# The sign bit of sixteen decoded weight pieces, set on another engine

## The chip, the cores and the metric

The kernel runs on one core of one Trainium2 chip. The metric is the device time of one execution in microseconds (us); the time before is 899.84 us, the median of 3 runs (899.83 to 900.71).

The engines that matter are TensorE (PE: matrix products), VectorE (DVE) and ScalarE (ACT), each with its own in-order queue of instructions, and the DMA queue of SyncE (SP), which loads inputs and stores the result. An instruction waits in its queue until semaphores say that what it reads has been written and that what it overwrites is no longer needed.

## The reference

Attention inside chunks of 64 rows, followed by a two-layer network whose activation is a rational function. The weights arrive as 64-bit floats, the rest as 32-bit floats.

```python
# attention, for each chunk of 64 rows, head_dim 64
scores = scale * q_c @ k_c.T
attn = softmax(scores)            # along the last axis, + 1e-9 in the divisor
x = attn @ v_c                    # 4608 tokens x 512
# network: w_in 512 x 2048, w_out 2048 x 512, a has 4 numbers, b has 2
h = x @ w_in
P = a[0] + a[1] * h + a[2] * h**2 + a[3] * h**3
Q = 1.0 + abs(b[0]) * abs(h) + abs(b[1]) * h**2
out = (P / (Q + 1e-06)) @ w_out   # float32
```

## The kernel before

**Tiling.** The 4608 tokens are 18 blocks n of 256. For each block there is one attention part, and then four steps s of 512 hidden columns. Steps are numbered g; for the first two blocks they alternate (g = 0 is block 0, step 0; g = 1 is block 1, step 0; g = 2 is block 0, step 1, and so on up to g = 7), after that they run block by block. A step g consists of the first product (`F g`, `f g` on TensorE, line 332, into the PSUM tile `ph`), the rational function, twelve instructions on ScalarE and VectorE with letters of their own (among them `p` and `P`, lines 360 and 364, of which `P` is VectorE's last read of `ph`; `g`, line 369, which writes `ghi`; `G`, line 381, which writes `glo`), and the second product (`Z g`, `z g` from `ghi`, `y g` from `glo`; line 407, into `po`). Each operand of a product is split into a high and a low part, and three products of the parts are summed.

**The weights.** They are decoded on the chip from the 64-bit floats. There are 16 pieces j of 128 x 1024 numbers, 8 of `w_in` and 8 of `w_out`, each loaded by one DMA (`w j`) into one of three buffers `raw` as pairs of 32-bit words, the low word first. A piece then goes through these instructions:

- `o j` (line 149, VectorE): the low word is shifted right by 29, which leaves its upper three bits;
- `s j` (line 153, ScalarE): the high word, read as a 32-bit float, is scaled by 2^-111. That moves its exponent and keeps its sign;
- the sign, in one of two ways. `i j` (line 157, ScalarE) converts the scaled high word to a 16-bit float and writes it into the upper half of the low word; the number is so small that only the sign is left of it. `e j` (line 161, VectorE) ands the high word with the sign mask and ors it into the low word, both 32 bits wide;
- `j j` (line 165, VectorE): the high word is shifted left by 3 and the low word ored in;
- `h j` (line 168, ScalarE): the high part for the products. The low part comes either from `d j` (line 173, VectorE) or from two products with identity matrices, `r j` on TensorE, and `l j` on ScalarE.

A `raw` buffer is free for the next load when `d j` or `r j` has read it.

**The order.** The first twelve steps are interleaved with the attention of blocks 0 to 3 and with the decoding by a table written out by hand, `START`: each entry is a letter and a piece, step or block number (with a half, as in `N0.1`), and the instructions are issued in the order of the table, each to the queue of its engine. Attention letters that matter here: `S` scores (TensorE, tile `pss`), `M` row maximum (VectorE, line 241), `U`, `E` and `n` subtraction, exponential and sums, `N` normalisation (VectorE, line 275), `T` transposition (TensorE, `pst`), `K` copy (ScalarE, line 288), `A` product with v (TensorE, `psx`), `X` and `Y` its high and low part (ScalarE, line 311, and VectorE, line 315). From step 12 on a loop issues the rest, without decoding.

In the table, pieces 1, 4, 2, 12, 7 and 10 take their sign by `e`, the other ten (3, 0, 5, 8, 6, 9, 13, 11, 14, 15) by `i`.

Of the kernel before, what the change touches and what calls it, by code (L numbers as in the profile page):

```python
# [13 lines left out]
ALU = mybir.AluOpType  # L14
# [16 lines left out]
EXP_WIDE = (0, 1)  # L31

START = (
# [12 lines left out]
)  # L46
FIRST = 12
CUT_FIRST, CUT_LAST = 24, 48
# [6 lines left out]
def tile_chunked_attention_rational_moe(  # L55
# [11 lines left out]
    nc = tc.nc  # L67
    cp = ctx.enter_context(tc.tile_pool(name="cp", bufs=1))
    p2 = ctx.enter_context(tc.tile_pool(name="p2", bufs=2))
# [14 lines left out]
    a0, a1, a2, a3 = (ab[:, i:i + 1] for i in range(4))  # L84
    b0, b1a = ab[:, 4:5], ab[:, 6:7]
# [36 lines left out]
    raws, pls = {}, {}  # L122
# [17 lines left out]
    def words(j):  # L140
        low, high = raws[j][:, :, 0], raws[j][:, :, 1]
        return low, high, high.bitcast(F32)
# [10 lines left out]
        nc.scalar.activation(val, val, AF.Copy, scale=2.0 ** -111)  # L153

    def w_sign(j):
        upper = raws[j].bitcast(mybir.dt.float16).rearrange("p f (w h) -> p f w h", h=2)[:, :, 0, 1]
        nc.scalar.copy(upper, words(j)[2])

    def w_sign_dve(j):
        low, high, _ = words(j)  # L160
        nc.vector.scalar_tensor_tensor(low, high, -(2 ** 31), low, ALU.bitwise_and, ALU.bitwise_or)  # L161

    def w_join(j):
        low, high, val = words(j)
# [297 lines left out]
    def qk(n, u=None):  # L462
# [5 lines left out]
    of_step = lambda f: lambda g: f(*steps[g])  # L468
    do = {
        "k": consts, "B": abs_b1, "q": qk, "v": load_v, "w": w_load,  # L470
        "o": w_low, "s": w_scale, "j": w_join, "i": w_sign, "e": w_sign_dve, "h": w_hi, "d": w_lo_dve, "r": w_rest, "l": w_lo,
        "S": att_s, "M": att_max, "U": att_sub, "E": att_exp, "n": att_rs, "N": att_norm,
        "T": att_t, "K": att_copy, "A": att_av, "X": att_xhi, "Y": att_xlo,
        "O": store,
# [22 lines left out]
    for g in range(FIRST, total + LAG):  # L497
        n, s = steps[min(g, total - 1)]
# [66 lines left out]
```

## Time and profile before

| | |
|---|---|
| median of the timed runs | 899.84 us (899.83 to 900.71) |
| span of the profiled execution, first to last instruction | 898.1 us |
| the profiled execution's own time | not listed apart from its span; the median is 1.7 us above the span |
| mean granted TensorE clock | 0.996 |
| busy time PE, PEld (weight loads) | 870.1 us, 854.2 us |
| busy time DVE, ACT | 748.0 us, 581.9 us |
| decoding: last instruction of it starts at | 129.4 us |

The profile is of one execution. A row of the timeline gives start, duration, engine, line, operation, what is written and read, and in brackets the idle time of the engine before it and what ended it. Durations of neighbours on one engine overlap by some tens of nanoseconds to a tenth of a microsecond, because the next instruction starts while the last one drains; what an instruction takes from its queue is therefore the distance from its start to the next start, called its slot below.

### The profile page before, as it was taken

How to read it: one execution, taken by the hardware profiler on the slowest of the kernel's cores; microseconds unless marked ns; L12 is line 12 of the kernel's file. 1: busy time of each engine (PE TensorE's matmuls, PEld its weight loads, DVE VectorE, ACT ScalarE, POOL GpSimd, SP SyncE). 2: the span in 40 equal slices, each digit the busy share in tenths (PEclk: the TensorE clock that was granted, in tenths of full speed). 3: DMA queues.
4: the chain of work that ended last, by engine and by line, in shares of the span. 5: the costliest groups of instructions: out<-in, count | busy, mean ns of one | idle time of the engine just before them, and what ended most of it. 6: DMA issues, size and time to landing. Idle time of an engine off the chain costs nothing.

```text
span 898.1 us, 21079 instructions
## 1 busy us (share of the span) xinstructions
PE 870.1 (97%) x9390; PEld 854.2 (95%) x9390; DVE 748.0 (83%) x671; ACT 581.9 (65%) x981; POOL 0.8 (0%) x8
## 2 busy tenths in 40 slices
PE   2699999999999999999999999999999999999998
PEld 2498999999999999999999999999999999999998
DVE  6999997898878878787878897878787878878784
ACT  6899987676656566665747475757565656566452
POOL 0000000000000000000000000000000000000000
PEclk9999999999999999999999999999999999999999
DMA  8525432103030303030201111020202030101010
GB/s 303 213 96 188 168 115 51 69 1 95 2 95 1 95 2 94 1 94 2 65 32 29 68 25 72 17 81 1 95 2 95 1 95 2 48 1 25 1 24 25
DMA packets 16506, 55.88 MB, mean 62 GB/s; under 512 B 2592, under 2 KB 2592, under 8 KB 14368
## 3 DMA queue, kind: packets, MB, share of 16 engines
q1 hardware_dynamic: 16256, 54.28, 18.5%
q8 instruction: 74, 1.21, 0.5%
q10 hardware_dynamic: 160, 0.26, 0.1%
q14 instruction: 16, 0.13, 0.0%
HBM read 45.09 MB, written 9.44 MB: 61 GB/s over the span
## 4 chain that ended last, share of the span: by engine, by line
PE 93%; DVE 3%; DMA 1%; ACT 1%; issue 1%; SPq 0%; ACTq 0%; DVEq 0%
PE ph L332 43%; PE po L407 42%; PE psx L205 2%; PE pss L205 2%; PE pst L284 2%; PE pe L407 1%; DMA Bqk<-in_kT 1%; PE pl L181 1%; DMA raw<-in_w_out 1%; DVE raw L165 0%; PE pe L432 0%; PE po L432 0%; DVE C L360 0%; DVE C L364 0%; DVE raw L161 0%
## 5 line engine op out<-in xcount | busy, mean ns | idle before, releaser
L332 PE MATMUL ph<-xhi,wi_hi 128*128 128x256 f32 x1152 | 322.7, 280 | 6.8 <-DVE C L364 6.8
L332 PE MATMUL ph<-xlo,wi_hi 128*128 128x256 f32 x1152 | 319.8, 278 | 0.0
L332 PE MATMUL ph<-xhi,wi_lo 128*128 128x256 f32 x1152 | 319.5, 277 | 0.0
L337 ACT ACTIVATE A<-ph,ab 128x1024 f32<-128x1024 f32 x72 | 80.7, 1121 | 253.9 <-PE ph L332 253.2
L332 PEld LDWEIGHTS ph<-xhi,wi_hi 128*128 128x128 f32 x1152 | 217.3, 189 | 8.3 <-ACT raw L153 7.5
L407 PE MATMUL po<-wo_hi,ghi 128*128 128x256 f32 (+1 forms) x1112 | 220.4, 280 | 0.0
L332 PEld LDWEIGHTS ph<-xlo,wi_hi 128*128 128x128 f32 x1152 | 217.7, 189 | 0.1
L332 PEld LDWEIGHTS ph<-xhi,wi_lo 128*128 128x128 f32 x1152 | 217.5, 189 | 0.0
L407 PE MATMUL po<-wo_lo,ghi 128*128 128x256 f32 x1112 | 217.1, 276 | 0.0
L348 DVE SCALAR_TENSOR_TENSOR B<-B,ab,A 128x1024 f32<-128x1024 f32 x72 | 92.4, 1283 | 99.0 <-ACT B L340 99.0
L407 PEld LDWEIGHTS po<-wo_hi,ghi 128*128 128x128 f32 x1112 | 167.6, 188 | 2.3 <-issue 0.3
L407 PEld LDWEIGHTS po<-wo_lo,ghi 128*128 128x128 f32 x1112 | 167.6, 188 | 0.0
L407 PE MATMUL po<-wo_hi,glo 128*128 128x256 f32 (+1 forms) x1112 | 138.1, 277 | 0.1
L407 PEld LDWEIGHTS po<-wo_hi,glo 128*128 128x128 f32 x1112 | 131.5, 188 | 0.3 <-DVE glo L381 0.3
L369 DVE SCALAR_TENSOR_TENSOR ghi<-C,ab,A 128x1024 fp32r<-128x1024 f32 x72 | 92.4, 1283 | 10.8 <-ACT A L356 2.4
L352 ACT ACTIVATE A<-B,cst 128x1024 f32<-128x1024 f32 x72 | 83.1, 1155 | 24.8 <-DVE B L348 24.7
L377 DVE SCALAR_TENSOR_TENSOR B<-C,ab,B 128x1024 f32<-128x1024 f32 x72 | 92.3, 1283 | 2.3
L364 DVE SCALAR_TENSOR_TENSOR C<-C,ab,ph 128x1024 f32<-128x1024 f32 x72 | 92.1, 1280 | 2.1
L381 DVE TENSOR_TENSOR glo<-B,A 128x1024 fp32r<-128x1024 f32 x72 | 88.2, 1224 | 6.6
L360 DVE TENSOR_TENSOR C<-C,ph 128x1024 f32<-128x1024 f32 x72 | 87.4, 1214 | 4.2 <-ACT B L340 3.6
L344 ACT ACTIVATE C<-ph,ab 128x1024 f32<-128x1024 f32 x72 | 87.6, 1216 | 4.5 <-PE ph L332 4.5
L373 DVE SCALAR_TENSOR_TENSOR B<-B,ghi 128x1024 f32<-128x1024 f32 x72 | 88.2, 1224 | 2.3
(72 smaller groups left out, 737.3 us busy)
## 6 DMA issues: line engine op xcount, KB each, us to landing
v<-in_vP SPq DMA_DIRECT2D x18, 512.0 KB, 4.1
out<-o SPq DMA_DIRECT2D x68, 128.0 KB, 2.4
raw<-in_w_in SPq DMA_DIRECT2D x8, 1024.0 KB, 6.1
raw<-in_w_out SPq DMA_DIRECT2D x8, 1024.0 KB, 4.8
qk<-in_qT SPq DMA_DIRECT2D x16, 512.0 KB, 4.8
qk<-in_kT SPq DMA_DIRECT2D x16, 512.0 KB, 5.6
Aqk<-in_qT SPq DMA_DIRECT2D x2, 256.0 KB, 5.3
Bqk<-in_kT SPq DMA_DIRECT2D x2, 256.0 KB, 5.8
```

The costliest lines, as they stand in the source:

```text
L332: nc.tensor.matmul(ph[:, fi, :], w[:, cc, f], x[:, cc, :], start=(k == 0), stop=(k == len(mm) - 1))
L337: nc.scalar.activation(ch[n, s][1], ch[n, s][0], AF.Abs, scale=b0)
L344: nc.scalar.activation(ch[n, s][3], ch[n, s][0], AF.Identity, bias=a2, scale=a3)
L348: nc.vector.scalar_tensor_tensor(B, B, b1a, A, ALU.mult, ALU.add)
L352: nc.scalar.activation(A, B, AF.Ln, bias=cst[:, 0:1], scale=2.0 ** -KLN)
L360: nc.vector.tensor_mul(C, C, h)
L364: nc.vector.scalar_tensor_tensor(C, C, a1, h, ALU.add, ALU.mult)
L369: nc.vector.scalar_tensor_tensor(gbuf[n, s][0], C, a0, A, ALU.add, ALU.mult)
L373: nc.vector.scalar_tensor_tensor(B, B, CQ, gbuf[n, s][0].bitcast(F32), ALU.add, ALU.mult)
L377: nc.vector.scalar_tensor_tensor(B, C, a0, B, ALU.add, ALU.subtract)
L381: nc.vector.tensor_mul(gbuf[n, s][1], B, A)
L407: nc.tensor.matmul(accs[n][i][:, cols], g[:, fi, i * 128:(i + 1) * 128], w[:, FPS * s + fi, cols], start=start, stop=stop,)
```

## The change

All 16 pieces now take their sign in one way. `i j` is a VectorE instruction with one operand: it reads the upper 16 bits of the high word as an integer, ands them with the sign mask, and writes them into the upper 16 bits of the low word. Elements are 16 bits wide, and successive ones are 8 bytes apart in reading and writing. `e` is gone, and in the table each `e j` is replaced by `i j` in its place; nothing else in the table changes (the diff shows it re-wrapped).

```diff
 START = (
...
-    ... w4 e1 T0.1 ... Y0.1 e4 j4 ... f0 e2 E1 ...
+    ... w4 i1 T0.1 ... Y0.1 i4 j4 ... f0 i2 E1 ...
...
     def w_sign(j):
-        upper = raws[j].bitcast(mybir.dt.float16).rearrange("p f (w h) -> p f w h", h=2)[:, :, 0, 1]
-        nc.scalar.copy(upper, words(j)[2])
-
-    def w_sign_dve(j):
-        low, high, _ = words(j)
-        nc.vector.scalar_tensor_tensor(low, high, -(2 ** 31), low, ALU.bitwise_and, ALU.bitwise_or)
+        half = raws[j].bitcast(mybir.dt.int16).rearrange("p f (w h) -> p f w h", h=2)
+        nc.vector.tensor_scalar(half[:, :, 0, 1], half[:, :, 1, 1], -(2 ** 15), None, ALU.bitwise_and)
...
-        "o": w_low, "s": w_scale, "j": w_join, "i": w_sign, "e": w_sign_dve, "h": w_hi, "d": w_lo_dve, "r": w_rest, "l": w_lo,
+        "o": w_low, "s": w_scale, "j": w_join, "i": w_sign, "h": w_hi, "d": w_lo_dve, "r": w_rest, "l": w_lo,
```

Four lines fewer stand ahead of what follows, so line 165 of before is line 161 after, line 364 is 360, and so on; line 157 is the new sign instruction.

VectorE's queue has 10 rows more, ScalarE's 10 fewer; PE's and SP's orders stay. Three places of VectorE's queue follow; numbers behind tile names tell buffers apart.

The first is early, during the attention of block 0: `raw_107` is piece 0, `raw_116` piece 1, `raw_86` piece 3; `e_111` being normalised is `N0.1`. Before:

```order
L173 SCALAR_TENSOR_TENSOR wi_lo<-raw_86,wi_hi 128x4x256
L275 TENSOR_TENSOR e_111<-e_111,sm_109 128x2x4x64
L161 SCALAR_TENSOR_TENSOR raw_116<-raw_116 128x1024
L165 SCALAR_TENSOR_TENSOR raw_107<-raw_107 128x1024
L165 SCALAR_TENSOR_TENSOR raw_116<-raw_116 128x1024
```

and now:

```order
L169 SCALAR_TENSOR_TENSOR wi_lo<-raw_86,wi_hi 128x4x256
L157 TENSOR_SCALAR raw_107<-raw_107 128x1024
L271 TENSOR_TENSOR e_111<-e_111,sm_109 128x2x4x64
L157 TENSOR_SCALAR raw_116<-raw_116 128x1024
L161 SCALAR_TENSOR_TENSOR raw_107<-raw_107 128x1024
L161 SCALAR_TENSOR_TENSOR raw_116<-raw_116 128x1024
```

The sign of piece 0 came from ScalarE's queue and now stands ahead of `N0.1`; the sign of piece 1 stays where it was, in the other form.

The second is the rational function of step 0, up to `P0` (the last row). `raw_265` is piece 5. Before:

```order
L275 TENSOR_TENSOR e_300<-e_300,sm_294 128x2x8x64
L348 SCALAR_TENSOR_TENSOR B_0_342<-B_0_342,ab,A_0_341 128x1024
L360 TENSOR_TENSOR C_0_345<-C_0_345,ph_0_268 128x1024
L165 SCALAR_TENSOR_TENSOR raw_265<-raw_265 128x1024
L364 SCALAR_TENSOR_TENSOR C_0_345<-C_0_345,ab,ph_0_268 128x1024
```

and now:

```order
L271 TENSOR_TENSOR e_300<-e_300,sm_294 128x2x8x64
L157 TENSOR_SCALAR raw_265<-raw_265 128x1024
L344 SCALAR_TENSOR_TENSOR B_0_342<-B_0_342,ab,A_0_341 128x1024
L356 TENSOR_TENSOR C_0_345<-C_0_345,ph_0_268 128x1024
L161 SCALAR_TENSOR_TENSOR raw_265<-raw_265 128x1024
L360 SCALAR_TENSOR_TENSOR C_0_345<-C_0_345,ab,ph_0_268 128x1024
```

The sign of piece 5 has come in ahead of the rational function of step 0.

The third is around `P3` (the last row), VectorE's last read of the `ph` tile of step 3. `raw_640` is piece 9, `raw_672` piece 10. Before:

```order
L369 SCALAR_TENSOR_TENSOR ghi_0_706<-C_0_642,ab,A_0_627 128x1024
L360 TENSOR_TENSOR C_1_682<-C_1_682,ph_1_600 128x1024
L373 SCALAR_TENSOR_TENSOR B_0_628<-B_0_628,ghi_0_706 128x1024
L149 TENSOR_SCALAR raw_672<-raw_672 128x1024
L364 SCALAR_TENSOR_TENSOR C_1_682<-C_1_682,ab,ph_1_600 128x1024
```

and now:

```order
L365 SCALAR_TENSOR_TENSOR ghi_0_706<-C_0_642,ab,A_0_627 128x1024
L356 TENSOR_TENSOR C_1_682<-C_1_682,ph_1_600 128x1024
L369 SCALAR_TENSOR_TENSOR B_0_628<-B_0_628,ghi_0_706 128x1024
L157 TENSOR_SCALAR raw_640<-raw_640 128x1024
L149 TENSOR_SCALAR raw_672<-raw_672 128x1024
L360 SCALAR_TENSOR_TENSOR C_1_682<-C_1_682,ab,ph_1_600 128x1024
```

The sign of piece 9 has come in two rows ahead of `P3`.

24 rows, old and new, of the table START are left out of this document.

## The prediction

> **What bounds the kernel now.** I read the page first, then the busy time by stages, then the chain that ended last, then the rows around the places where TensorE waits.
>
> ```profile
> span 898.1 us, 21079 instructions
> PE 870.1 (97%) x9390; PEld 854.2 (95%) x9390; DVE 748.0 (83%) x671; ACT 581.9 (65%) x981; POOL 0.8 (0%) x8
> ```
>
> TensorE is busy for 870.1 of 898.1 us, so the time is its work plus 28 us of idling. Shares over the whole span hide where that lies; the stages show it (columns: busy us of PE, PEld, DVE, ACT, POOL, with instruction counts, then the granted clock, the DMA share and GB/s):
>
> ```profile
> 10.00:44.00 34.00, 19.14 (x229) 13.68 (x230) 31.86 (x39) 29.81 (x30) 0.00 (x0) 0.96 0.68 257
> 44.00:78.00 34.00, 34.00 (x307) 31.53 (x307) 33.90 (x33) 32.51 (x31) 0.00 (x0) 0.94 0.43 148
> 78.00:131.00 53.00, 53.00 (x555) 51.48 (x554) 52.75 (x51) 48.99 (x68) 0.00 (x0) 1.00 0.38 145
> 131.00:176.00 45.00, 45.00 (x496) 44.60 (x495) 36.09 (x33) 31.47 (x58) 0.00 (x0) 1.00 0.20 60
> 176.00:898.00 722.00, 717.78 (x7779) 711.94 (x7777) 591.11 (x515) 436.87 (x797) 0.00 (x0) 1.00 0.13 40
> ```
>
> From 44 us on TensorE hardly idles. VectorE is full from 10 to 131 us: it idles 2.14 us in the first of these stages (34.00 - 31.86), 0.10 in the second and 0.25 in the third. ScalarE is well filled too, but has 4.2, 1.5 and 4.0 us free. So while the weights are decoded VectorE is the engine without room, and from 131 us on it has plenty (8.9 us idle of 45). What VectorE gains or loses in the decoding reaches the end only where TensorE waits for it. The longest such wait, and its two sides:
>
> ```profile
> PE ph L332 <- DVE C L364: 6.8, 1, 6.8
> ...
> 42.31 1.27 DVE L364 SCALAR_TENSOR_TENSOR C<-C,ab,ph 128x1024 f32<-128x1024 f32 x1
> ...
> 43.73 0.55 PE L332 MATMUL ph<-xhi,wi_hi 128*128 128x256 f32 x1 [6.84 <-DVE C L364]
> ```
>
> `P0` on VectorE ends at 42.31 + 1.27 = 43.58, and 0.15 us later TensorE starts `F2`, which needs that `ph` tile. I take 0.15 us as the distance from a VectorE end to the TensorE start that it releases.
>
> **The change part by part.** The five decoding groups as they are (duration in ns: least, median, most):
>
> ```profile
> L149 DVE TENSOR_SCALAR raw<-raw x16: 643/687/696, 9.1 to 122.7; 128x1024 int32<-128x1024 int32 x16
> L153 ACT ACTIVATE raw<-raw x16: 1112/1185/1385, 9.1 to 118.0; 128x1024 f32<-128x1024 f32 x16
> L165 DVE SCALAR_TENSOR_TENSOR raw<-raw x16: 1212/1220/1226, 13.8 to 126.9; 128x1024 int32<-128x1024 int32 x16
> L157 ACT CAST raw<-raw x10: 2474/2608/2690, 10.7 to 124.0; 128x1024 f16<-128x1024 f32 x10
> ...
> L161 DVE SCALAR_TENSOR_TENSOR raw<-raw x6: 1214/1219/1227, 18.9 to 87.2; 128x1024 int32<-128x1024 int32 x6
> ```
>
> Removed from ScalarE: 10 x 2.608 = 26.1 us. Of this I count nothing: VectorE idles only 2.14 + 0.10 + 0.25 = 2.5 us between 10 and 131 us, so an earlier ScalarE can hardly release it earlier, and TensorE's wait above ends on VectorE. What covers it is VectorE's own queue; if that cover went, the most to come back would be these 2.5 us.
>
> On VectorE six two-operand signs go and sixteen new ones come. What counts is the slot:
>
> ```profile
> 18.25 0.68 DVE L275 TENSOR_TENSOR e<-e,sm 128x512 f32<-128x512 f32 x1
> 18.85 1.22 DVE L161 SCALAR_TENSOR_TENSOR raw<-raw 128x1024 int32<-128x1024 int32 x1
> 19.99 1.22 DVE L165 SCALAR_TENSOR_TENSOR raw<-raw 128x1024 int32<-128x1024 int32 x1
> ...
> 60.44 0.69 DVE L149 TENSOR_SCALAR raw<-raw 128x1024 int32<-128x1024 int32 x1
> 61.04 1.27 DVE L364 SCALAR_TENSOR_TENSOR C<-C,ab,ph 128x1024 f32<-128x1024 f32 x1
> ```
>
> An old sign takes 19.99 - 18.85 = 1.14 us of the queue. The new one is not in the trace. Its nearest row is L149: the same operation with one operand and a constant, the same 1024 elements at the same 8-byte steps, in place, only 32 bits wide; its slot is 61.04 - 60.44 = 0.60 us. The nearest rows that write 16-bit elements at 8-byte steps are ScalarE's L157, 2.2 times as long as L153 with 32 bits, and its slot is here:
>
> ```profile
> 77.79 2.63 ACT L157 CAST raw<-raw 128x1024 f16<-128x1024 f32 x1
> 80.07 1.30 ACT L153 ACTIVATE raw<-raw 128x1024 f32<-128x1024 f32 x1
> ...
> L249 DVE TENSOR_SCALAR sm<-sm x16: 170/174/177, 107.8 to 802.2; 128x16 f32<-128x16 f32 x16
> ```
>
> So 80.07 - 77.79 = 2.28 us is the upper end for the new slot. For the lower end: L249, the same operation on 16 elements, lasts 0.174 us, so of L149's 0.687 some 0.51 is for the elements; at twice the rate the slot would be about 0.60 - 0.26 = 0.34 us. I call the slot s and take s = 0.60, after L149, because engine, operation, count and steps agree, and L157 differs in engine.
>
> VectorE's total grows by 16 x 0.60 - 6 x 1.14 = 2.8 us. Where it arrives:
>
> ```profile
> 19.08 1.09 PE L284 MATMUL pst<-ident,e 128*128 128x128 f32 x4 [3.98 <-DVE e L275]
> ...
> 27.82 1.16 PE L205 MATMUL pss<-Bqk,Aqk 64*64 64x64 f32 x64
> ...
> 29.05 1.23 DVE L241 TENSOR_REDUCE sm<-pss 128x16 f32<-128x1024 f32 x1
> ```
>
> *Up to the restart of TensorE.* The sign of piece 3 falls into VectorE's idle time at 10 us (the wait for ScalarE's exponential), nothing. The sign of piece 0 stands ahead of `N0.1` (the row at 18.25), which TensorE's `T0.1` waits for at 19.08. Everything behind hangs on that as a chain (copy, product with v, high part, correction product, then `S1`): `S1` ends at 27.82 + 1.16 = 28.98, now + 0.60 = 29.58, and `M1`, at 29.05 before, is late by 0.53. (The pieces 1 and 4 are cheaper, but `M1` waits for `S1` now.) Behind `M1` VectorE runs without a gap: piece 2 gives back 1.14 - 0.60 = 0.54, piece 5 ahead of step 0 adds 0.60. `P0` and with it `F2` come 0.53 - 0.54 + 0.60 = **0.59 us** late.
>
> *From there to 131 us* TensorE and VectorE both run without gaps, and TensorE is late by the most that VectorE's delay exceeds the slack at a place where it takes something from VectorE:
>
> ```profile
> 78.49 1.27 DVE L364 SCALAR_TENSOR_TENSOR C<-C,ab,ph 128x1024 f32<-128x1024 f32 x1
> ...
> 79.95 0.31 PE L332 MATMUL ph<-xhi,wi_hi 128*128 128x256 f32 x1
> ...
> 116.93 1.22 DVE L381 TENSOR_TENSOR glo<-B,A 128x1024 fp32r<-128x1024 f32 x1
> ...
> 119.32 4.02 PE L407 MATMUL po<-wo_hi,glo 128*128 128x256 f32 x32
> ...
> 130.52 1.22 DVE L381 TENSOR_TENSOR glo<-B,A 128x1024 fp32r<-128x1024 f32 x1
> 132.36 1.22 DVE L360 TENSOR_TENSOR C<-C,ph 128x1024 f32<-128x1024 f32 x1 [0.62 <-ACT A L337]
> 133.50 1.22 DVE L315 TENSOR_TENSOR xlo<-psx,xhi 128x1024 fp32r<-128x1024 f32 x1
> 134.68 1.28 DVE L364 SCALAR_TENSOR_TENSOR C<-C,ab,ph 128x1024 f32<-128x1024 f32 x1
> ...
> 135.45 1.16 PE L205 MATMUL pss<-qk 64*64 64x64 f32 x64
> 136.54 0.39 PE L332 MATMUL ph<-xhi,wi_hi 128*128 128x256 f32 x1
> ...
> 148.48 1.22 DVE L360 TENSOR_TENSOR C<-C,ph 128x1024 f32<-128x1024 f32 x1 [2.11 <-ACT B L340]
> ```
>
> - `P3` (78.49) ends at 79.76; `F5` starts at 79.95: slack 0.04 after the 0.15. Pieces 12, 8, 7, 6, 9 lie between: -0.54 + 0.60 - 0.54 + 0.60 + 0.60 = 0.72, so `P3` is late by 1.31 and `F5` by 1.27.
> - `G4` (116.93) ends at 118.15; `y4` starts at 119.32: slack 1.02. Pieces 13, 10, 11, 14 add 1.26, 2.57 in all; `y4` late by 1.55.
> - Piece 15 makes it 3.17. `p6` started at 132.36 although VectorE was free at 130.52 + 1.13; those 0.71 us are absorbed, 2.46 remain. `Y2` (133.50) ends at 134.72 and releases `S3` at 135.45: slack 0.58, late by 1.88. `P6` ends at 135.96, `F8` starts at 136.54: slack 0.43, late by **2.03**.
>
> The other places where TensorE takes something from VectorE before 131 us have more slack, read off in the same way. Afterwards VectorE's idle time (2.11 us before the row at 148.48) takes up the delay, and VectorE follows TensorE. TensorE has no such idle time, so 2.03 us stay to the end. SP's order stays: a weight load starts when L173 or the correction product has released its buffer, and that shifts with its VectorE readers. For any s between 0.60 and 2.28 the same walk gives 13 s - 5.77.
>
> Span 898.1 + 2.0 = 900.1; the same 1.7 us as now between span and median give 899.84 + 2.03 = **901.9 us**.
>
> **The rivals.** *The 16-bit store is slow on VectorE too.* For it: L157 is the only 16-bit row with these steps and is 2.2 times as long as its 32-bit neighbour. Against: another engine, and L165, L149 and L153 do not suffer from 8-byte steps. At 2.2 x 0.60 = 1.32, 13 s - 5.77 = 11.4 us, 911.2 us; at one element a pass like the two-operand forms, s = 1.14, 9.1 us, 908.9; at ScalarE's own 2.28, 23.9 us, 923.7. [...]
>
> *Not slower: 16 bits run at double rate.* Then s = 0.34: `F2` would come at 3 x 0.34 - 1.21 = -0.2, the later places gain as well, and TensorE's own work holds the rest: 899.7 us. By 13 s - 5.77 the delay falls under 1.80 us, 0.2%, from s = 0.58 down. For it: the data are half as wide. Against: the sum of L149 is for elements, and the elements are as many and as far apart. [...]
>
> *ScalarE's relief counts.* If VectorE's idle 2.14 us before 44 went with it, the restart would come 1.55 us early instead of 0.59 late; the 1.44 us that come later (2.03 - 0.59) come all the same, in all -0.1, 899.7 us. I put it with the last.
>
> **How the numbers follow.** A measurement of this kernel tells 0.2% (1.8 us) from no change. Forecast, s near 0.60 (0.55 to 0.67, with the slacks read to some tenths): 901.0 to 903.0, chance 0.60, of which two thirds lie above 901.64 (0.40 slower, 0.20 same). Slow 16-bit stores: 0.22 for 909 to 911, 0.10 for 920 and more, all slower. Not slower, both ways: 0.08 (0.05 same, 0.03 faster). Together slower 0.72, same 0.25, faster 0.03. The range leaves out the 0.10 at the top and most of the 0.08 at the bottom: 900.2 to 911.3.
>
> **What would show it.** In the profile after: the duration of line 157 on DVE (0.69 for the forecast; 1.2 and more for the first rival, about 0.43 for the second); `F2`'s start near 44.3 instead of 43.73; new waits of `ph` line 328 at `F5` and `F8` for line 360; VectorE without gaps to about 134; ScalarE's busy time less by 26. The forecast is wrong if line 157 lasts something else, or if VectorE's slots elsewhere change once ScalarE stops writing 16-bit halves beside it.

## The result and the profile after

| | before | after |
|---|---|---|
| median of the timed runs | 900.24 us (899.83 to 900.71) | 909.12 us (908.89 to 909.62) |
| span of the profiled execution | 898.1 us | 907.1 us |
| sign on VectorE, median of one | 1.219 us (6, two-operand) | 1.342 us (16, 16-bit) |
| sign on ScalarE, median of one | 2.608 us (10) | none |
| VectorE, ScalarE busy over the span | 748.0, 581.9 us | 759.4, 559.7 us |

The ratio is 1.0098, 95% interval 1.0085 to 1.0112: slower by 8.9 us. (The 900.24 us are the median of four runs of the kernel before, one more than the 899.84 us above.) The new instruction and its neighbours in the decoding, as the view of the tile `raw` groups them after the change (least, median, most in ns):

```profile
L149 DVE TENSOR_SCALAR raw<-raw x16: 644/692/767, 8.9 to 132.1; 128x1024 int32<-128x1024 int32 x16
L157 DVE TENSOR_SCALAR raw<-raw x16: 1292/1342/1376, 10.1 to 133.9; 128x1024 int16<-128x1024 int16 x16
L161 DVE SCALAR_TENSOR_TENSOR raw<-raw x16: 1206/1226/1285, 13.9 to 137.4; 128x1024 int32<-128x1024 int32 x16
```

The same operation on the same 1024 elements at the same 8-byte steps lasts twice as long with 16-bit elements (line 157, 1.342 us) as with 32-bit ones (line 149, 0.692), and longer than the two-operand form (line 161, 1.226). Its slot, from the timeline after:

```profile
33.20 1.36 DVE L157 TENSOR_SCALAR raw<-raw 128x1024 int16<-128x1024 int16 x1
34.59 1.23 DVE L161 SCALAR_TENSOR_TENSOR raw<-raw 128x1024 int32<-128x1024 int32 x1
...
40.17 1.29 DVE L157 TENSOR_SCALAR raw<-raw 128x1024 int16<-128x1024 int16 x1
41.26 1.25 DVE L344 SCALAR_TENSOR_TENSOR B<-B,ab,A 128x1024 f32<-128x1024 f32 x1
...
121.44 1.34 DVE L157 TENSOR_SCALAR raw<-raw 128x1024 int16<-128x1024 int16 x1
122.55 1.25 DVE L369 SCALAR_TENSOR_TENSOR B<-B,ghi 128x1024 f32<-128x1024 f32 x1
```

The last two are 1.09 and 1.11 us, and all but two lie between 1.08 and 1.16; I use 1.12. The two are pieces 4 and 2, whose join `j` stands directly behind the sign: 1.37 and 1.39 us (the first pair of rows is piece 2), where the old sign took 1.26 and 1.25. At 1.12 each, the sixteen add 16 x 1.12 - 6 x 1.14 = 11.1 us to VectorE's queue. The stages after, in the columns of before:

```profile
10.00:44.00 34.00, 17.68 (x228) 12.90 (x228) 32.66 (x40) 20.77 (x25) 0.00 (x0) 0.94 0.69 259
44.00:78.00 34.00, 31.47 (x279) 28.84 (x280) 33.90 (x32) 25.40 (x25) 0.00 (x0) 0.91 0.30 105
78.00:131.00 53.00, 49.42 (x458) 46.95 (x457) 52.83 (x52) 38.52 (x64) 0.00 (x0) 1.00 0.39 142
131.00:176.00 45.00, 44.28 (x546) 43.48 (x544) 37.50 (x36) 29.30 (x56) 0.00 (x0) 1.00 0.30 95
176.00:907.00 731.00, 726.78 (x7855) 720.94 (x7853) 600.17 (x522) 443.29 (x803) 0.00 (x0) 1.00 0.13 40
```

VectorE is as full as before (33.90 of 34, 52.83 of 53). ScalarE fell from 32.51 to 25.40 and from 48.99 to 38.52, and nothing became faster by it. TensorE, which had no idle time from 44 to 176 us, now idles 2.5, 3.6 and 0.7 us there. The granted clock from 44 to 78 us reads 0.91 instead of 0.94, but that is no part of the loss: TensorE still stands idle for the first 2 us of that stage, and behind its restart the clock is 0.50 up to 50.1 us, for 4.0 us, against 4.4 us before (43.73 to 48.1). At single places, in the timeline of TensorE after, and two groups of its waits (us in total, times, longest):

```profile
46.11 0.55 PE L328 MATMUL ph<-xhi,wi_hi 128*128 128x256 f32 x1 [9.12 <-DVE C L360]
...
85.91 0.35 PE L328 MATMUL ph<-xhi,wi_hi 128*128 128x256 f32 x1 [1.29 <-DVE C L360]
...
144.87 1.16 PE L201 MATMUL pss<-qk 64*64 64x64 f32 x64
145.96 0.39 PE L328 MATMUL ph<-xhi,wi_hi 128*128 128x256 f32 x1
...
PE pst L280 <- DVE e L271: 6.0, 2, 5.1
PE po L403 <- DVE wo_lo L169: 1.1, 2, 0.7
```

`F2` starts 2.38 us late (43.73 before), `F5` 5.96 us (79.95), `S3` and `F8` 9.42 us (135.45 and 136.54), and the span ends 9.0 us late, so 0.4 us are made up behind `F8`. The loss grows through the decoding, piece by piece, and stops where the decoding stops.

### The profile page after: what moved, and what is told of

The parts are those of the page before. It is cut to its first block, busy times and chain, and to the rows that moved or that the text cites. A ratio compares the mean times of both kernels' runs of the same rounds, so it can differ in the third digit from the quotient of the medians.

```text
span 907.1 us, 21078 instructions
## 1 busy us (share of the span) xinstructions
PE 870.8 (96%) x9390; PEld 854.1 (94%) x9390; DVE 759.4 (84%) x681; ACT 559.7 (62%) x971; POOL 0.8 (0%) x8
## 3 DMA queue, kind: packets, MB, share of 16 engines
q8 instruction: 74, 1.21, 0.6%
## 4 chain that ended last, share of the span: by engine, by line
PE 82%; DVE 13%; issue 2%; ACT 1%; DMA 1%; SPq 0%; DVEq 0%; ACTq 0%
PE ph L328 38%; PE po L403 38%; PE psx L201 2%; DVE raw L157 2%; PE pss L201 2%; DVE raw L161 2%; PE pst L280 2%; DVE C L356 1%; DVE B L344 1%; DVE B L369 1%; DVE C L360 1%; DVE ghi L365 1%; DVE glo L377 1%; PE pe L403 1%; DVE raw L149 1%
```

## The experiments

Two questions: is the size of the new slot the whole cause, and why is the slot 1.12 us instead of 0.60. "Before" in each ratio is the kernel before, run on the same chip.

**Whole words in the same places.**

```diff
-        nc.vector.tensor_scalar(half[:, :, 0, 1], half[:, :, 1, 1], -(2 ** 15), None, ALU.bitwise_and)
+        nc.vector.tensor_scalar(low, high, -(2 ** 31), None, ALU.bitwise_and)
```

> The sign instruction keeps its 16 places, its operation and its waits, but takes whole 32-bit words (the sign bit replaces the low word, so the lowest three bits of every weight are left out). Theory A, the slot of the 16-bit instruction is what was mis-sized and the walk is right: its slot falls to that of the shift of the low word, 0.60 us, line 157 lasts 0.69 us, the first product of step 2 starts near 44.3 us, and the time is 13 x 0.60 - 5.77 = 2.0 us above before, about 902. Theory B, the places or the waits of the new instructions cost the time, whatever their length: it stays near 909.

Measured: 901.62 us, ratio 1.0017 (1.0008 to 1.0026). Line 157 and the two restarts in its profile:

```profile
L157 DVE TENSOR_SCALAR raw<-raw x16: 687/692/698, 10.1 to 126.4; 128x1024 int32<-128x1024 int32 x16
...
43.61 0.55 PE L328 MATMUL ph<-xhi,wi_hi 128*128 128x256 f32 x1 [6.96 <-ACT A L352]
...
80.54 0.35 PE L328 MATMUL ph<-xhi,wi_hi 128*128 128x256 f32 x1 [0.72 <-DVE C L360]
```

Of the 8.9 us, 7.4 are gone with nothing changed but the width of what is read and written: sixteen instructions in the same places with the same waits. Theory B falls. Even so 1.5 us remain, so a sign at half the price of now still loses against before. One detail of the walk was wrong: `F2` is not late at all (43.61). It starts 0.14 us after the end of `P0` (42.19 + 1.28 = 43.47), as before; line 352, which the row names, ends 0.03 us ahead of it.

**16-bit elements, but closer together.**

```diff
-        nc.vector.tensor_scalar(half[:, :, 0, 1], half[:, :, 1, 1], -(2 ** 15), None, ALU.bitwise_and)
+        nc.vector.tensor_scalar(half[:, :512, :, 1], half[:, :512, :, 1], -1, None, ALU.bitwise_and)
```

> The changed kernel with its 16 instructions at their places, still 1024 elements of 16 bits each, but at 4-byte steps: each takes the upper halves of the first 1024 words of the piece and writes them back unchanged, so no sign is set. If the 16-bit store costs by the 16-byte stretches that it touches, half as many are touched: line 157 lasts 0.74 us, its slot is near 0.65 us, and the time is 901.5 to 903 (13 x 0.65 - 5.77 = 2.7 above before, or 0.6 less, as with whole words). If 16-bit elements as such are slow: 909.

Measured: 901.86 us, ratio 1.0016 (1.0006 to 1.0025).

```profile
L157 DVE TENSOR_SCALAR raw<-raw x16: 729/774/802, 9.9 to 127.3; 128x1024 int16<-128x1024 int16 x16
```

So 16-bit elements as such are not slow; the same count at 4-byte steps lasts 0.77 us, against 1.34 at 8-byte steps. The mean granted clock of the profiled execution is 0.994 here too, as in the changed kernel, so the clock is not what made the loss there.

**32 bits read, 16 bits written.**

```diff
-        nc.vector.tensor_scalar(half[:, :, 0, 1], half[:, :, 1, 1], -(2 ** 15), None, ALU.bitwise_and)
+        nc.vector.tensor_copy(upper, words(j)[2])
```

> The sign is still written as 16 bits at 8-byte steps, but what is read is the 32-bit high word (VectorE converts it to a 16-bit float, as ScalarE did in the kernel before). If the 16-bit write is what is slow: line 157 lasts 1.3 us as now and the time stays near 909. If the 16-bit read is what is slow, or the two-halves operation as such: line 157 lasts 0.69 us and the time is near 902.

Measured: 909.03 us, ratio 1.0099 (1.0083 to 1.0114).

```profile
L157 DVE CAST raw<-raw x16: 1295/1338/1371, 10.2 to 134.0; 128x1024 f16<-128x1024 f32 x16
```

The write is what costs; how wide the read is makes no difference (1.338 us here, 1.342 in the changed kernel).

**Single forms.** They stand behind the end of the kernel before, where nothing else runs.

```diff
+    for _ in range(2):
+        nc.vector.tensor_scalar(at(dst[I16], 4), at(src[I16], 4), -2 ** 15, None, ALU.bitwise_and)
+        nc.vector.tensor_scalar(at(dst[I32], 2), at(src[I32], 2), -2 ** 15, None, ALU.bitwise_and)
+        nc.vector.tensor_scalar(at(dst[I16], 2), at(src[I16], 2), -2 ** 15, None, ALU.bitwise_and)
...
+        nc.scalar.copy(at(dst[F16], 4), at(src[F32], 2))
...
```

> The kernel before with 28 instructions behind its end, on 1024 elements a partition, that measure single forms, twice each. On VectorE: a bitwise and with 16-bit elements at 8-byte steps (as in the change), with 32-bit at 8 bytes, with 16-bit at 4 and at 2 bytes, with 16-bit read at 8 and written at 2 bytes and the other way round, with 32-bit at 4 bytes; then copies from 32-bit at 8 bytes to 16-bit at 8 bytes, to 16-bit at 2 bytes, and to 32-bit at 8 bytes. On ScalarE: copies from 32-bit at 8 bytes to 16-bit at 8, 4 and 2 bytes and to 32-bit at 8 bytes. If a lone 16-bit write is what is slow, on whichever engine: all forms that write 16 bits at 8 bytes last about 1.3 us on VectorE and 2.5 us on ScalarE, those that write 16 bits at 2 bytes at most 0.69 and 1.2 us, and reading at 8 bytes costs nothing. If VectorE takes all 16-bit elements with steps one a pass: the forms that only read them at 8 bytes last 1.2 us too.

The timeline of VectorE and of ScalarE there (lines 542 to 545 are the bitwise and with 16 bits at 8-byte steps, 32 bits at 8, 16 bits at 4, 16 bits at 2; 546 reads 16 bits at 8 and writes at 2; 547 reads at 2 and writes at 8; 548 has 32 bits at 4, as neighbours; 552 to 555 are ScalarE's copies to 16 bits at 8, 4 and 2 bytes and to 32 bits at 8):

```profile
903.88 1.30 DVE L542 TENSOR_SCALAR bdst<-bench 128x1024 int16<-128x1024 int16 x1 [14.50 <-DMA bdst<-in_kT]
905.21 0.69 DVE L543 TENSOR_SCALAR bdst<-bench 128x1024 int32<-128x1024 int32 x1
905.94 0.74 DVE L544 TENSOR_SCALAR bdst<-bench 128x1024 int16<-128x1024 int16 x1
906.71 0.43 DVE L545 TENSOR_SCALAR bdst<-bench 128x1024 int16<-128x1024 int16 x1
907.17 0.69 DVE L546 TENSOR_SCALAR bdst<-bench 128x1024 int16<-128x1024 int16 x1
907.90 1.30 DVE L547 TENSOR_SCALAR bdst<-bench 128x1024 int16<-128x1024 int16 x1
909.24 0.69 DVE L548 TENSOR_SCALAR bdst<-bench 128x1024 int32<-128x1024 int32 x1
...
912.76 2.46 ACT L552 CAST bdst<-bench 128x1024 f16<-128x1024 f32 x1 [17.60 <-DVE bdst L551]
915.25 1.33 ACT L553 CAST bdst<-bench 128x1024 f16<-128x1024 f32 x1
916.61 1.09 ACT L554 CAST bdst<-bench 128x1024 f16<-128x1024 f32 x1
917.73 1.09 ACT L555 COPY bdst<-bench 128x1024 f32<-128x1024 f32 x1
```

Writing 16 bits at 8-byte steps takes 1.30 us on VectorE, whether they are read so (542) or as neighbours (547), and 2.46 on ScalarE. Reading them so and writing neighbours (546) takes 0.69, which is 0.26 more than neighbours on both sides (545) and as much as 32-bit words take (543, 548). So the first form of the expectation holds for the store; that reading at 8-byte steps costs nothing holds only against 32-bit words. It is the same store that is slow on both engines, and the 2.6 us of the old ScalarE copy have the same cause as the 1.34 us of the new instruction.

**By what the store costs.** The same place, with half as many elements and other steps.

```diff
+        one(half(dst, I16, 2), half(src, I16, 1))
+        one(half(dst, I16, 4), half(src, I16, 1))
+        one(half(dst, I16, 8), half(src, I16, 1))
...
```

> The kernel before with single forms behind its end: on VectorE 512 elements of 16 bits written at 4, 8 and 16-byte steps, 512 of 32 bits written at 8 and 16-byte steps, and 1024 of 16 bits written as 512 adjacent pairs at 8 and 16-byte steps; on ScalarE 512 of 16 bits at 8 and 16-byte steps and 512 of 32 bits at 16. If a lone 16-bit write costs by the 8-byte word that it touches: 8 and 16 bytes alike near 0.7 us on VectorE, 4 bytes near 0.45, 32-bit writes near 0.43 at both steps, pairs as fast as 32-bit writes. If the step alone costs, whatever the width: 16-byte steps are slower than 8-byte ones for 32 bits too.

VectorE's timeline (16 bits at 4, 8 and 16-byte steps, 32 bits at 16, 16-bit pairs at 8 and at 16), and ScalarE's (16 bits at 8 and 16-byte steps, 32 bits at 16):

```profile
903.61 0.45 DVE L542 TENSOR_SCALAR bdst<-bench 128x512 int16<-128x512 int16 x1 [13.45 <-DMA bdst<-in_qT]
...
904.10 0.73 DVE L542 TENSOR_SCALAR bdst<-bench 128x512 int16<-128x512 int16 x1
...
906.11 1.30 DVE L542 TENSOR_SCALAR bdst<-bench 128x512 int16<-128x512 int16 x1 [1.28 <-DMA bdst<-in_kT]
...
907.90 0.62 DVE L542 TENSOR_SCALAR bdst<-bench 128x512 int32<-128x512 int32 x1
...
908.56 0.43 DVE L542 TENSOR_SCALAR bdst<-bench 128x1024 int16<-128x1024 int16 x1
...
909.02 0.62 DVE L542 TENSOR_SCALAR bdst<-bench 128x1024 int16<-128x1024 int16 x1
...
909.67 1.32 ACT L552 CAST bdst<-bench 128x512 f16<-128x512 f32 x1 [13.72 <-DVE bdst L542]
911.03 2.46 ACT L553 CAST bdst<-bench 128x512 f16<-128x512 f32 x1
913.51 1.09 ACT L554 COPY bdst<-bench 128x512 f32<-128x512 f32 x1
```

Neither form of the expectation explains the 16-bit stores. 512 elements at 16-byte steps last 1.30 us, as long as 1024 at 8-byte steps, and 512 at 8-byte steps 0.73, as long as 1024 at 4-byte steps (0.74). So neither the elements count nor the 8-byte words that they touch. What these pairs share is the memory that they spread over, 8 KB of a partition in the first and 4 KB in the second pair. Counted in stretches of 16 bytes, the largest step run, 512 and 256 are written to, and (1.30 - 0.73) / 256 is 2.2 ns for each, as an estimate; for ScalarE, 2.46 and 1.32 in the same pairs, it is 4.4 ns. That the stretch is 16 bytes long is not shown: no run has a step above 16 bytes, and longer stretches would fit as well. 32-bit words lost less by the step: on VectorE 512 at 16-byte steps last 0.62 against 0.43 at 8, and two 16-bit halves side by side last the same (0.62 and 0.43 for 1024). On ScalarE 512 words of 32 bits at 16-byte steps last 1.09, as long as 1024 at 8-byte steps.

**One part of the change alone.** Only the ten ScalarE copies exchanged, then only the six two-operand signs.

```diff
     def w_sign(j):
-        nc.scalar.copy(upper, words(j)[2])
+        nc.vector.tensor_scalar(half[:, :, 0, 1], half[:, :, 1, 1], -(2 ** 15), None, ALU.bitwise_and)
```

> Only the ten ScalarE copies become 16-bit VectorE instructions; the six two-operand signs stay. Theory A: the six exchanges are 1.14 us against 1.12 us of queue and do nothing, so all of the loss is here: 909. If the exchange of the six carries a part of the loss, by new waits say, the time is below 908.

```diff
     def w_sign_dve(j):
-        nc.vector.scalar_tensor_tensor(low, high, -(2 ** 31), low, ALU.bitwise_and, ALU.bitwise_or)
+        nc.vector.tensor_scalar(half[:, :, 0, 1], half[:, :, 1, 1], -(2 ** 15), None, ALU.bitwise_and)
```

> Only the six two-operand signs become 16-bit instructions; the ten ScalarE copies stay. Theory A: no change, 899.5 to 900.8. Theory B, the new form costs by more than its slot: some us above 901.

Measured: ten alone 908.85 us, ratio 1.0092 (1.0078 to 1.0105); six alone 900.69 us, 1.0006 (0.9997 to 1.0015). The ten carry the loss; the six are an even exchange as far as the interval tells.

**ScalarE loaded again.**

```diff
+    def w_extra():
+        for _ in range(5):
+            nc.scalar.copy(scratch, ident.unsqueeze(1).to_broadcast([P, 2, P]))
```

> The changed kernel, and at the ten places where ScalarE's sign copies stood it is given five small copies into a scratch tile that nobody reads, about 2.2 us together, so that it is as loaded as before. If ScalarE's relief was worth nothing: 909 to 909.8, as the changed kernel. If the relief gave something back that hid a larger loss, up to the 2.5 us that VectorE idled between 10 and 131 us: up to 911.6.

Measured: 909.29 us, ratio 1.0104 (1.0087 to 1.0121). Its stages from 10 to 131 us:

```profile
10.00:44.00 34.00, 18.88 (x228) 13.41 (x228) 32.72 (x40) 26.57 (x39) 0.00 (x0) 0.98 0.67 250
44.00:78.00 34.00, 31.38 (x283) 28.74 (x284) 33.90 (x32) 29.26 (x35) 0.00 (x0) 0.92 0.33 118
78.00:131.00 53.00, 49.01 (x454) 46.39 (x453) 52.83 (x52) 45.75 (x84) 0.00 (x0) 1.00 0.39 140
```

ScalarE is busy for 26.57 + 29.26 + 45.75 = 101.6 us, against 84.7 in the changed kernel and 111.3 before, so about two thirds of the load that it lost are back, and the time is the same. ScalarE's relief was worth nothing that can be measured.

**The sign twice.**

```diff
         nc.vector.tensor_scalar(half[:, :, 0, 1], half[:, :, 1, 1], -(2 ** 15), None, ALU.bitwise_and)
+        nc.vector.tensor_scalar(half[:, :, 0, 1], half[:, :, 1, 1], -(2 ** 15), None, ALU.bitwise_and)
```

> The changed kernel with each of the 16 sign instructions issued twice. Theory A (the walk): s is the two slots together, 1.12 + 1.15 to 1.25 since the second follows the first on the same words, so 2.3: 13 x 2.3 - 5.77 = 24.1 above before, 923 to 926. Rival: part of the 909 is a cost paid once, of the first late wait, and the second instruction costs only where TensorE already waits: 909 + 13 x 1.12 = 923.7 at most, and below 918 if the idle time behind it takes part of it up.

Measured: 930.21 us, ratio 1.0345 (1.0324 to 1.0366), 4 us above the range of theory A; the rival is out. The two slots are 1.33 and 1.10 us, s = 2.43, and 13 x 2.43 - 5.77 = 25.8 against 30.0. The rest appears ahead of the restart:

```profile
53.66 0.55 PE L329 MATMUL ph<-xhi,wi_hi 128*128 128x256 f32 x1 [12.56 <-DVE C L361]
```

`F2` is 9.9 us late where the walk gives 3 x 2.43 - 1.21 = 6.1. The walk leaves out pieces 3, 1 and 4, since other waits cover them. For pieces 1 and 4 that holds as long as a sign is no longer than the 1.14 us it replaces; here they add 2 x (2.43 - 1.14) = 2.6 us. The signs of piece 3 leave VectorE 1.56 us late (`j3` starts at 15.34, before at 13.78). Some 0.5 us of the two are taken up by idle time on the way, and `M1` is 6.14 us late (35.19, before 29.05) where the walk has 2.36.

**An attempt at something faster.** For the six pieces, ScalarE writes the sign as 32-bit zeros, and VectorE's shift takes it in.

```diff
+    def w_mark(j):
+        nc.scalar.activation(w_dest(j)[1], grid(words(j)[2], j), AF.Copy, scale=2.0 ** -100)
+
+    def w_low_sign(j):
+        low = grid(words(j)[0], j)
+        mark = w_dest(j)[1].bitcast(I32)
+        nc.vector.scalar_tensor_tensor(low, low, 29, mark, ALU.logical_shift_right, ALU.bitwise_or)
```

> The kernel before, with another sign for the six pieces that VectorE signs: ScalarE writes the sign as a 32-bit zero with sign into the place where the piece's low part will stand (about 1.1 us each), and VectorE's shift of the low word takes it in as its second operand (1.14 us), so the shift of its own (0.60 us) goes. No 16-bit store is added. Theory A (what VectorE's queue holds sets the time): VectorE is 0.60 us shorter per piece; the pieces 1 and 2 stand ahead of the restart, so the first product of step 2 starts 1.2 us earlier, and the time is 1.2 us below before, 0.9987. Rival: ScalarE, with 6.6 us more to do, is waited for, and the time is that of before or above.

As far as its output tells, this kernel leaves out the signs of the six pieces; the zeros that ScalarE writes were not read, and where the signs are lost is open. The instructions and their waits are the ones meant. Measured: 904.11 us, ratio 1.0044 (1.0031 to 1.0056). A miss for theory A, and the rival is right:

```profile
10.00:44.00 34.00, 18.84 (x228) 13.39 (x228) 28.16 (x34) 30.75 (x31) 0.00 (x0) 0.96 0.69 259
...
27.96 1.23 DVE L159 SCALAR_TENSOR_TENSOR raw<-raw,wo_lo 128x1024 int32<-128x1024 int32 x1 [1.49 <-ACT wo_lo L154]
```

VectorE is busy for 3.7 us less in the first stage (28.16 against 31.86). Three shifts of 0.60 us are gone, and the rest is work that has moved behind the stage, since the shift now waits for two ScalarE instructions in a row. `F2` starts at 45.70, 2.0 us late. Behind it the granted clock stays low for longer: from 44 to 78 us it reads 0.89 (0.94 before), and the products of the restart follow each other at 0.21 us up to 51.6 us, for 5.9 us (before up to 48.1, for 4.4 us), and at 0.11 to 0.12 us after that. How much of the other 1.5 us that makes was not worked out. With `P0` moved ahead:

```diff
-    ... d2 c0 w12 N1 b0 i5 Q0 w8 p0 I0 j5 s12 m12 P0 J0 F2 ...
+    ... d2 c0 w12 p0 P0 N1 b0 i5 Q0 w8 I0 j5 s12 m12 J0 F2 ...
```

> As the run before, and VectorE's two instructions on the first product of step 0 (the last of which releases the restart) stand ahead of the normalisation of block 1, the sign-free join of piece 5 and the first quotient, some 3.5 us earlier. Theory A: the restart comes about 4 us earlier than in the kernel before, but step 5 and step 8 of the products still wait for VectorE's total, which is 2.4 us and 3.0 us shorter there: 2.4 us below before, 0.997. Rival: TensorE's idle time sets the end by itself: 4 us or more below.

Measured: 906.58 us, ratio 1.0069 (1.0055 to 1.0082). `P0` ends at 42.41 instead of 45.55 in the run before, but `b0`, ScalarE's read of the same `ph` tile, stands behind it in the table, waits for it and then holds the restart (43.52). That is 0.2 us earlier than in the kernel before, and the run is 6.0 us slower all the same, a miss for both forms of the expectation. It is lost behind the restart:

```profile
44.00:78.00 34.00, 31.08 (x274) 28.74 (x274) 29.73 (x27) 33.83 (x30) 0.00 (x0) 0.91 0.27 97
78.00:131.00 53.00, 51.73 (x529) 49.16 (x527) 51.48 (x50) 51.40 (x73) 0.00 (x0) 1.00 0.39 148
...
53.13 1.32 PE L282 MATMUL pst<-ident,e 128*128 128x128 f32 x8 [2.12 <-ACT wo_lo L186]
```

TensorE, which had no idle time here before, idles 2.9 us in the first and 1.3 us in the second stage, the longest time for a low part that ScalarE writes (2.12 us), and the granted clock reads 0.91 in the first stage, where it was 0.94. ScalarE is now the full engine (33.83 of 34). Neither version beats the kernel before.

## Why the prediction was right, and where not

- **What bounds the decoding** was right. VectorE's queue sets the time up to 131 us: the load of ScalarE changes nothing (909.29 us with 101.6 us of it, 909.12 with 84.7), and the time follows line 157's slot (901.6 at 0.60, 901.9 at about 0.65, 909.1 at 1.12, 930.2 at 2.43; the 0.65 is an estimate, the 0.77 us that one lasts less an overlap between the 0.1 of the 32-bit forms and the 0.2 of the changed kernel).
- **The direction** was right: sixteen slots of VectorE against six lose at any price tried, also at 0.60 us, where 1.5 us remain of the 2.0 forecast.
- **The size of the term was wrong**: s was taken as 0.60 after L149 "because engine, operation, count and steps agree, and L157 differs in engine". That the store is slow does not hang on the engine, only how slow it is (1.30 and 2.46 us). Its width and step decide here (1024 elements on VectorE last 1.30 us with 16 bits at 8-byte steps, 0.74 at 4, and 0.69 with 32 bits at 8), and of the two nearest rows L157 was the one that showed them, on ScalarE. s is 1.12 us.
- **The first rival** was right: the 16-bit store is slow on VectorE too. Its 2.2 x 0.60 = 1.32 us is close to the 1.34 us that one lasts; as a slot that is too much, since the next instruction overlaps by 0.2 us (1.34 against the slot of 1.12; 0.1 for the 32-bit forms). Its s = 1.14 gives 908.9, and 909.12 was measured, but the reason that it gives, one element a pass as in the two-operand forms, is shown by no run: what the trace has of those is their slot, 1.14 us, and 16-bit elements at 4-byte steps last 0.74 us, little more than 32-bit ones (0.69). That its number fits is luck.
- **The walk** held as a sum: 13 x 1.12 - 5.77 = 8.8 us, measured 8.9. Of its steps, `F5` is 5.96 us late where it gives 8 x 1.12 - 3.53 = 5.43, and `F8` 9.42 for 8.8. One step is wrong: that piece 0's delay passes through `T0.1` to `S1` and `M1`. In the run with whole words `T0.1` starts 0.54 us late (19.62), yet `S1` starts at 27.58, earlier than before (27.82). The correction products in between take up the delay: the second pair of line 181 (177 there) takes 1.91 us before and 1.23 there, although the granted clock reads 1.00 in both; why is open. That is most of the 0.5 to 0.7 us by which `F2` and the end came out better than the walk in that run. In the changed kernel `S1` is on time too (27.91), but VectorE itself reaches `M1` 1.28 us late (30.33). In its own queue `N0.1` already starts 1.25 us late (19.50, before 18.25), by the sign of piece 0 and by the 0.17 us that the sign of piece 3 exceeds its idle time, and at 1.12 us pieces 1 and 4 give nothing back. So the delay of one sign that the walk has at `M1` came by another way than it says, and that the sum fits is in part luck.
- **Two more points of the walk.** Between `F5` and `F8` TensorE does not wait where it says (`y4`, `S3`, `F8`): it waits 0.41 and 0.72 us for low parts of `w_out` that VectorE writes (line 169), 0.89 us for the normalisation of block 2 (line 271) and 0.20 us for line 245, places that the prediction does not list. The other 1.25 of the 3.46 us that are added there are not idle time: TensorE is busy for 57.84 us between the two, 56.59 before, and why is open. And 13 s - 5.77 does not hold up to 2.28: above 1.14 us pieces 1 and 4 add to it, and the sign issued twice came out 4.2 us above it, so the 923.7 us of the first rival is too low.
- **The second and third rival** (double rate, ScalarE's relief) are out: no run shows s = 0.34, since the 0.43 us that the rival had were measured for 16-bit neighbours at 2-byte steps alone, while 1024 elements last 0.74 us at 4-byte and 1.30 at 8-byte steps, and ScalarE's load has no effect on the time (909.29 against 909.12 us). ScalarE's busy time fell by 22.2 us and not by 26, since the 26.1 sum durations: ten slots of 2.28 are 22.8.
- **The range** held the time, in the upper part that the first rival had put there. The forecast inside it, 901.0 to 903.0 with a chance of 0.60, missed.

The rows behind the step at `S1` and `M1`, before, with whole words, and after the change:

```profile
25.66 1.91 PE L181 MATMUL pl<-raw,ident 128*128 128x512 f32 x2
...
19.62 1.09 PE L280 MATMUL pst<-ident,e 128*128 128x128 f32 x4 [4.58 <-DVE e L271]
26.20 1.23 PE L177 MATMUL pl<-raw,ident 128*128 128x512 f32 x2
27.58 1.16 PE L201 MATMUL pss<-Bqk,Aqk 64*64 64x64 f32 x64
...
19.50 0.72 DVE L271 TENSOR_TENSOR e<-e,sm 128x512 f32<-128x512 f32 x1
30.33 1.22 DVE L237 TENSOR_REDUCE sm<-pss 128x16 f32<-128x1024 f32 x1
```

## What to carry to other kernels

Before an instruction is priced from a row with the same engine and operation, look for a row that has the same width and step of its output, on whichever engine: where one store of a kernel lasts twice as long as the instructions beside it (here 2.608 us on ScalarE, against 1.185 of the scaling), the store may be the reason and not the engine. An engine that is full and that the bound waits for gained nothing here from relief of another one (909.12 us with ScalarE relieved, 909.29 with two thirds of its load back); what a change adds to its queue arrives at the end in large part (8.9 of 11.1 us here, 1.5 of 2.8 with whole words), up to the first stage where it idles. And a walk through the tight places gives the slope well, but the places it leaves out as covered came back when the term grew (4.2 us above it at s = 2.43).

## What the hardware showed that was not expected

- Stores of single 16-bit elements that are not neighbours took a time that goes with the memory they spread over and not with their number. Over 8 KB of a partition (1024 at 8-byte or 512 at 16-byte steps) they lasted 1.30 us on VectorE and 2.46 on ScalarE, over 4 KB (1024 at 4-byte or 512 at 8-byte steps) 0.73 to 0.74 and 1.32 to 1.33. Worked out from these, each 16 bytes take 2.2 and 4.4 ns, an estimate; steps above 16 bytes were not run. Reading 1024 at 8-byte steps and writing neighbours took VectorE 0.69 us, as 32-bit words did, against 0.43 for neighbours on both sides.
- On VectorE, 1024 whole 32-bit words written at 8-byte steps took as long as neighbours (0.69 us in both), and 512 at 16-byte steps lasted 0.62 against 0.43 us at 8.
